# First expert unit: tokens chosen a tile earlier, rows turned inside attention's last two tiles, the end of routing spread over more steps

## The chip, the cores and the metric

The kernel runs on one core of one Trainium2 chip. The metric is the device time of one execution in microseconds (us); lower is better. The kernel before took 1397.6 us, the median of three runs from 1397.01 to 1399.13. One core has five instruction streams that work side by side: TensorE (PE, matmuls, with PEld for its weight loads), VectorE (DVE), ScalarE (ACT), GpSimd (POOL, which also issues the indirect DMAs) and SyncE (SP, which only issues DMAs). A trailing q, as in SPq or ACTq, marks an engine's own queue of issues and waits. Streams wait for each other by semaphores.

## The reference

Three layers, one after the other, on 4608 tokens of 512 numbers (8 batches of 576, 8 heads of 64):

```python
# 1: retention attention, no softmax
ret = (q @ k.T / 8) * Dmat          # Dmat[i,j] = gamma_head**(i-j) for i>=j, else 0
x   = (ret @ v), heads side by side # [4608, 512]
# 2: a mixture of 8 experts, one expert for each token
logits = x @ w_gate + modality_bias[modality_id]
e_idx  = argmax(logits); gate = softmax(logits)[e_idx]
y[tok] = gate * (relu(x[tok] @ w1[e]) @ w2[e])   # 512 -> 1024 -> 512
# 3: a dense block
h = y @ w_in; out = (h - tanh(h)) @ w_out        # 512 -> 2048 -> 512
```

## The kernel before

All matmuls carry fp32 in two pieces, a rounded high part and a low part, as three passes (high by high, high by low, low by high). There are three stages.

**Attention and routing.** The loop over t runs over 36 tiles of 128 tokens. The step of tile t issues scores(t+1) (L362; DVE masks the scores into `a`, L366), attend(t) (L398 with the carried state, L406 with `a` and the scaled values `vs` that POOL makes, L421 the new state, which ACT copies at L425), and evac_x(t) (DVE, L431), which puts the tile's output into `xt`, a buffer for a group of four tiles. Routing of a group g of four tiles comes in three parts, a tile apart, after the group is complete: route_a (logits on PE, L462, copied to `ls` by ACT, L465), route_b (transposes, L471, and the argmax on DVE, L475 to L487, into `oh_all`) and route_c (ranks, L496 to L501 on PE, then slots and counts on DVE, L504 to L514). Behind it, tile by tile, scatter writes the token numbers into a list of slots in DRAM (POOL, L517 and L518, tile `slot_d`), and store_x turns the rows (turn_x, L529), scales them (ACT, L534, tile `xo`) and writes them to `x_d` in DRAM (L536). `due` delays the scatters of group 6 so that they come in two halves.

**The first expert's tokens.** When seven of the nine groups are counted (EARLY = 7), choose() (L437 on PE, L441 to L453 on DVE) picks the expert with the most tokens so far. SP reads the pick into registers (L607, L608), load_ids (L199) reads 400 slot entries into `idt0`, and gather_rows (L203, POOL) fetches 128, 128, 128 and 16 rows of `x_d`, here into two buffers `vk` of the attention's pool. Once attention is done, turn_rows transposes each block of rows (L161 on PE into `sc` or `xp`), ACT writes the high part `xh` (L162) and DVE the low part `xl` (L163).

**Expert units.** A unit is 400 tokens of one expert, in eight steps f. A step has 12 matmuls of gemm1 (L712, 512 to 128 hidden) and, two steps behind, 12 of gemm2 (L933 to L935). The weights of a step come by DMA into `raw` (load_raw, L781), and split_w cuts them into `wh` (ACT, L790) and `wl` (DVE, L791). After gemm1 of a step, post() makes `hi` (ACT, L822) and `lo` (DVE, L823), splits the next weights and loads later ones, and then prep() does work that fills in. In unit 0 prep does the end of routing: rest_a at f = 0 (last scatters of group 7, route_b of group 8), rest_b at f = 1 (route_c of group 8, two late stores, four scatters), rest_c at f = 2 (L640, the counts summed; table(), L660 to L683, 23 small DVE instructions that lay out all further units; four late stores). Then swap() exchanges the buffer pools; SP reads the table, load_ids fetches the ids of unit 1 at f = 2, its rows are gathered at f = 3 (L203, tile `xg`) and turned at f = 6 and 7.

**Dense block.** From about 600 us to the end PE multiplies without a break.

Each engine runs its instructions in the order in which this code issues them. Memory is assigned by the order in which pools and tiles are opened: `raw` lies on bytes that the attention's `vk`, `vs` and `a` used.

Of the kernel before, what the change touches and what calls it, by code (L numbers as in the profile page):

```python
# [8 lines left out]
F32 = mybir.dt.float32  # L9
# [21 lines left out]
RG = 4  # L31
# [84 lines left out]
def kernel(tc, A, out):  # L116
    nc = tc.nc
    with ExitStack() as ctx:
# [132 lines left out]
        with tc.manual_schedule():  # L251
            c1, c1r = ExitStack(), ExitStack()
            p1, p1r = pools(c1), pools(c1r)
# [10 lines left out]
            ps_m = p1r("ps_m", 2, space=PSUM, side="right")  # L264
# [38 lines left out]

            load_tile(0)
# [268 lines left out]
            for t in range(NTILE):  # L573
                g, r = divmod(t, RG)
                if t + 1 < NTILE:
                    scores(t + 1)
                attend(t)
# [13 lines left out]
                if t >= RG + 3:  # L591
                    for w in due(t - RG - 3):
                        scatter(w)
                if g >= 1:
                    if r == 0:
                        ls_box[g - 1] = route_a(g - 1)
                    elif r == 1:
                        route_b(g - 1, ls_box.pop(g - 1))
                    elif r == 2:
                        route_c(g - 1)  # L600
# [3 lines left out]
                if t == (EARLY + 1) * RG - 1:  # L604
                    choose()
                if t == (EARLY + 1) * RG + 1:
# [4 lines left out]
                    x0 = [gld.tile([128, 2, DM], F32, name="vk") for _ in range(SE // 2)]  # L611
                    x0 = [x0[s // 2][:, s % 2] for s in range(SE)]
# [9 lines left out]
            def early(s):  # L622
                turn_rows(0, s, x0[s], ps_sc.tile([128, KD, TL], F32, name="sc") if s < 3 else ps_x.tile([128, 2, KD, TL], F32, name="xp")[:, 0])

            def rest_a():
                for i in range(3):
                    scatter(NTILE - RG - 3 + i)
                route_b(g, ls_last)
                save_x(t_ahead, tp_ahead, True)
                late_x(1)  # L630

            def rest_b():
                route_c(g)
                late_x(2)
                for r in range(RG):
                    scatter(g * RG + r)

            def rest_c():
                cp = ps_m.tile([128, E], F32, name="m")
                nc.tensor.matmul(out=cp, lhsT=ones, rhs=cum[:, NRG], start=True, stop=True)  # L640
                table(cp)
                late.extend(range(g * RG, NTILE))
                late_x(RG)
# [41 lines left out]
            early(0)  # L685
            early(1)
            ls_last = route_a(g)
            for s in range(2, SE):
                early(s)
            t_ahead = late.pop(0)  # L690
            tp_ahead = turn_x(t_ahead, False)
# [56 lines left out]
            with ExitStack() as c2:  # L748
# [69 lines left out]
                def post(i, hp, ht):  # L818
                    if hp is None:
                        return  # L820
                    hi, lo = (ht_p.tile([128, UL], F32R, name=n)[:, 0:UE] for n in ("hi", "lo"))
# [244 lines left out]
```

## Time and profile before

| | |
|---|---|
| runs | 1397.6 us median (1397.01 to 1399.13) |
| profiled execution | 1397.72 us, its span 1396.0 us |
| busy share of the span | PE 97%, DVE 75%, ACT 50%, POOL 24% |
| scores of the last tile begin / first gemm1 begins | 143.41 / 154.06 us |
| gemm1 of unit 0, step 3, ends / rows of unit 1 turned from | 172.31 / 185.28 us |

The profile is of one execution. Its page names the busy time of each engine, and the trace behind it gives the start, the length and the wait ahead of each instruction: `[0.67 <-ACT wh L790]` behind a row says that the engine sat idle for 0.67 us just before it, and that the last thing it waited for was ACT writing `wh` at line 790. Matmuls overlap by their fill, so a row's length is longer than the distance to the next row. Times in us count from the start of the span.

### The profile page before, as it was taken

The page shows a single profiled execution, that of the slowest core. Times are in us where ns is not written, and L with a number is a line of the kernel's source. Part 1 is how long each engine was busy: PE and PEld are TensorE (multiplying, and loading weights), DVE is VectorE, ACT ScalarE, POOL GpSimd, SP SyncE. Part 2 cuts the span into 40 slices and gives each one's busy share as a digit, 9 for nine tenths or more (in the row PEclk, how much of TensorE's full clock was granted, in tenths as well). Part 3 has the DMA queues.
Part 4 walks back from the last instruction along what each step waited for, and adds up shares of the span by engine and source line. Part 5 has one row for each costly group of instructions (what it writes and reads, how often), then busy time and mean ns, then how long its engine had stood idle before and what let it go on. Part 6 is the DMA issues. An engine that isn't in the chain of part 4 may idle for free.

```text
span 1396.0 us, 22342 instructions
## 1 busy us (share of the span) xinstructions
PE 1358.1 (97%) x8267; PEld 1185.8 (85%) x8267; DVE 1048.7 (75%) x1684; ACT 695.9 (50%) x1232; POOL 337.3 (24%) x381
## 2 busy tenths in 40 slices
PE   8999899999989999999999999999999999999998
PEld 7887798999989999988888888888888888888886
DVE  5766677888888888658878778787787877778775
ACT  3323444444434444446656555555555555565553
POOL 4555353343334444010011100111001110011101
PEclk9999999999999999999999999999999999999999
DMA  9997647444743336634000000000000000000000
GB/s 372 404 332 280 207 151 210 125 132 137 221 126 94 95 94 165 119 128 154 31 31 31 31 1 31 31 31 31 1 31 31 31 31 0 31 31 0 31 1 31
DMA packets 79858, 141.06 MB, mean 101 GB/s; under 512 B 36224, under 2 KB 42944, under 8 KB 79744
## 3 DMA queue, kind: packets, MB, share of 16 engines
q1 hardware_dynamic: 58912, 84.23, 19.3%
q10 hardware_dynamic: 12096, 35.45, 7.2%
q0 software_dynamic: 8736, 19.90, 4.5%
q8 instruction: 66, 1.08, 0.3%
q14 instruction: 48, 0.39, 0.1%
HBM read 133.33 MB, written 39.80 MB: 124 GB/s over the span
## 4 chain that ended last, share of the span: by engine, by line
PE 51%; issue 5%; POOL 0%; POOLq 0%; ACT 0%
PE hp L712 26%; PE acc L1010 8%; PE acc L1012 8%; PE acc L1011 8%; POOL out_dram L1036 0%; POOLq L1062 0%; ACT o L1033 0%; POOL nopt L1035 0%; POOLq L1026 0%; POOLq L1036 0%
## 5 line engine op out<-in xcount | busy, mean ns | idle before, releaser
L983 ACT ACTIVATE eh<-hp 128x512 f32<-128x512 f32 x144 | 86.4, 600 | 293.0 <-PE hp L712 276.0
L712 PE MATMUL hp<-xh,winh 128*128 128x512 f32 x576 | 224.2, 389 | 0.1
L1010 PE MATMUL acc<-wout,hi 128*128 128x512 f32 x576 | 224.2, 389 | 0.0
L1012 PE MATMUL acc<-wout,lo 128*128 128x512 f32 x576 | 224.2, 389 | 0.0
L1011 PE MATMUL acc<-wout,hi 128*128 128x512 f32 x576 | 224.1, 389 | 0.0
L712 PE MATMUL hp<-xh,winl 128*128 128x512 f32 x576 | 224.1, 389 | 0.0
L712 PE MATMUL hp<-xl,winh 128*128 128x512 f32 x576 | 224.1, 389 | 0.0
L985 DVE TENSOR_TENSOR el<-eh,hp 128x512 f32<-128x512 f32 x144 | 99.1, 688 | 156.4 <-ACT eh L984 156.4
L194 POOL DMA_INDIRECT xg<-x_d,idt x130 | 155.6, 1197 | 216.8 <-DVE cv_a L235 70.5
L740 POOL TENSOR_TENSOR xl<-yr,xh 128x512 fp32r<-128x512 f32 x36 | 49.2, 1367 | 429.7 <-ACT xh L739 429.7
L933 PE MATMUL acc<-hi,wh 128*128 128x400 f32 x384 | 132.6, 345 | 16.3 <-ACT yo L912 16.3
L994 DVE SCALAR_TENSOR_TENSOR el<-eh,el 128x512 f32<-128x512 f32 x144 | 128.5, 893 | 15.4 <-DVE el L993 0.5
L712 PE MATMUL hp<-xh,wl 128*128 128x400 f32 x384 | 133.2, 347 | 4.3 <-DVE wl L791 4.0
L791 DVE TENSOR_TENSOR wl<-raw,wh 128x1024 fp32r<-128x1024 f32 (+1 forms) x98 | 117.7, 1202 | 24.4 <-ACT wh L790 23.0
L712 PE MATMUL hp<-xh,wh 128*128 128x400 f32 x384 | 131.7, 343 | 1.2 <-ACT wh L790 0.7
L712 PE MATMUL hp<-xl,wh 128*128 128x400 f32 x384 | 131.5, 342 | 0.8 <-DVE xl L163 0.8
L934 PE MATMUL acc<-lo,wh 128*128 128x400 f32 x384 | 131.3, 342 | 0.0
L935 PE MATMUL acc<-hi,wl 128*128 128x400 f32 x384 | 131.3, 342 | 0.0
L712 PEld LDWEIGHTS hp<-xh,winh 128*128 128x128 f32 x576 | 108.2, 188 | 22.9 <-issue 0.5
L1012 PEld LDWEIGHTS acc<-wout,lo 128*128 128x128 f32 x576 | 108.1, 188 | 22.8 <-DVE lo L989 0.4
L1011 PEld LDWEIGHTS acc<-wout,hi 128*128 128x128 f32 x576 | 108.2, 188 | 22.5
L712 PEld LDWEIGHTS hp<-xh,winl 128*128 128x128 f32 x576 | 108.1, 188 | 22.6
(169 smaller groups left out, 2541.4 us busy)
## 6 DMA issues: line engine op xcount, KB each, us to landing
raw<-in_w_dram SPq DMA_DIRECT2D x91, 512.0 KB
qk<-in_qk_dram SPq DMA_DIRECT2D x36, 512.0 KB
vk<-in_vk_dram SPq DMA_DIRECT2D x36, 512.0 KB
y_d<-yo SPq DMA_DIRECT2D x12, 800.0 KB
yr<-y_d SPq DMA_DIRECT2D x9, 1024.0 KB
raw<-in_wo_dram ACTq DMA_DIRECT2D x16, 512.0 KB
wo_d<-cv_em ACTq DMA_DIRECT2D x16, 512.0 KB
raw<-in_wi_dram ACTq DMA_DIRECT2D x16, 512.0 KB
```

What stands on the lines that cost most here:

```text
L194: nc.gpsimd.indirect_dma_start(out=dst, out_offset=None, in_=x_d[0:NT, :].rearrange("t (q c) -> (t q) c", q=NQ), in_offset=bass.IndirectOf ...
L712: nc.tensor.matmul(out=hp, lhsT=lhs, rhs=rhs, start=j == 0, stop=j == 3 * KD - 1)
L791: nc.vector.tensor_tensor(out=wl[:, 0:n], in0=r, in1=wh[:, 0:n].bitcast(F32), op=ALU.subtract)
L933: nc.tensor.matmul(out=o, lhsT=wh[:, cs], rhs=hi, start=first, stop=False)
L934: nc.tensor.matmul(out=o, lhsT=wh[:, cs], rhs=lo, start=False, stop=False)
L935: nc.tensor.matmul(out=o, lhsT=wl[:, cs], rhs=hi, start=False, stop=last)
L983: nc.scalar.activation(out=u, in_=hp, func=ACTF.Square)
L985: nc.vector.tensor_tensor(out=v, in0=u, in1=hp, op=ALU.mult)
L994: nc.vector.scalar_tensor_tensor(out=v, in0=s, scalar=SQ_C, in1=v, op0=ALU.add, op1=ALU.mult)
L1010: nc.tensor.matmul(out=acc[s], lhsT=hi, rhs=wh, start=first, stop=False)
L1011: nc.tensor.matmul(out=acc[s], lhsT=hi, rhs=wl, start=False, stop=False)
L1012: nc.tensor.matmul(out=acc[s], lhsT=lo, rhs=wh, start=False, stop=last)
```

## The change

The chain for group 6 runs a tile earlier: route_a right behind scores(29) in the step of tile 28, route_b in that step, route_c at 29, the scatters two a tile at 29, 30 and 31 (the tile before brings one), choose() at 30 instead of 31, and the loads and gathers at 32 instead of 33. The rows go to a buffer `xt` instead of two `vk`. Their first block is transposed after scores(35) and before attend(34), the next two before attend(35), and the last, of 16 rows, after attention. In the opening of unit 0 the three raw loads come first, then split_w of step 0, the late turn_x, the last block of rows, route_a of group 8, and split_w of steps 1 and 2. rest_b moves from f = 1 to f = 2, with route_c of group 8 ahead of it in post() of that step; rest_c, swap and the ids of unit 1 move from f = 2 to f = 3; late stores are two each at f = 1, 2 and 3. The turning of unit 1's rows stays at f = 6 and 7. The pool `ps_m` has its own stack, `acc` is opened at f = 2, and two unused pairs of `qk` and `vk` tiles are allotted at the start.

```diff
@@ -249,8 +249,8 @@
             return load, [(COST[0], lambda: (p0(), p1())), (COST[1], p2), (COST[2], p3), (COST[3], p4)], save
 
         with tc.manual_schedule():
-            c1, c1r = ExitStack(), ExitStack()
-            p1, p1r = pools(c1), pools(c1r)
+            c1, c1r, c1m = ExitStack(), ExitStack(), ExitStack()
+            p1, p1r, p1m = pools(c1), pools(c1r), pools(c1m)
             att = p1("att", 1)
             gld = p1("gld", AHEAD)
             tmp = p1("tmp", 2)
@@ -261,7 +261,7 @@
             ps_sc = p1("ps_sc", 3, space=PSUM)
             ps_x = p1("ps_x", 1, space=PSUM)
             ps_st = p1("ps_st", 1, space=PSUM)
-            ps_m = p1r("ps_m", 2, space=PSUM, side="right")
+            ps_m = p1m("ps_m", 2, space=PSUM, side="right")
 
             mask = att.tile([128, 2, TL], F32, name="mask")
             gx = att.tile([128, PERIOD, H // 2, TL], F32, name="gx")
@@ -301,6 +301,9 @@
                 if w < TL:
                     nc.scalar.copy(out=gx[:, r, :, w:TL], in_=gx[:, 0, :, 0:TL - w])
 
+            for _ in range(AHEAD - 4):
+                gld.tile([128, 2, H // 2, TL], F32, name="qk")
+                gld.tile([128, 2, DM], F32, name="vk")
             load_tile(0)
             nc.gpsimd.memset(mask, 1.0)
             for m in range(2):
@@ -572,8 +575,16 @@
 
             for t in range(NTILE):
                 g, r = divmod(t, RG)
+                soon = g == EARLY
                 if t + 1 < NTILE:
                     scores(t + 1)
+                if soon and r == 0:
+                    ls_box[g - 1] = route_a(g - 1)
+                if t == NTILE - 2:
+                    turn_rows(0, 0, x0[0], ps_sc.tile([128, KD, TL], F32, name="sc"))
+                if t == NTILE - 1:
+                    for s in range(1, SE - 1):
+                        turn_rows(0, s, x0[s], ps_m.tile([128, KD, TL], F32, name="m"))
                 attend(t)
                 evac_x(t)
                 if t + 4 < NTILE:
@@ -588,28 +599,42 @@
                     make_gx(t + 1)
                 if 2 <= t < 5:
                     clear_slots(t - 2)
-                if t >= RG + 3:
-                    for w in due(t - RG - 3):
+                if t >= RG + 3 and not soon:
+                    w = t - RG - 3
+                    if w // RG != EARLY - 1:
                         scatter(w)
                 if g >= 1:
                     if r == 0:
-                        ls_box[g - 1] = route_a(g - 1)
+                        if not soon:
+                            ls_box[g - 1] = route_a(g - 1)
+                        else:
+                            route_b(g - 1, ls_box.pop(g - 1))
+                            scatter(t - RG - 3)
                     elif r == 1:
-                        route_b(g - 1, ls_box.pop(g - 1))
+                        if not soon:
+                            route_b(g - 1, ls_box.pop(g - 1))
+                        else:
+                            scatter(t - RG - 3)
+                            scatter(t - RG - 2)
+                            route_c(g - 1)
                     elif r == 2:
-                        route_c(g - 1)
+                        if not soon:
+                            route_c(g - 1)
+                    if soon and r >= 2:
+                        for w in range(t - RG - 2 + r - 2, t - RG + r - 2):
+                            scatter(w)
                     for w in due(t - RG - 2):
                         if w // RG < NRG - LATE:
                             store_x(w)
-                if t == (EARLY + 1) * RG - 1:
+                if t == EARLY * RG + 2:
                     choose()
-                if t == (EARLY + 1) * RG + 1:
+                if t == (EARLY + 1) * RG:
                     base = nc.sync.value_load(pick[0:1, 0:1], min_val=0, max_val=(E - 1) * CAP)
                     first = nc.sync.value_load(pick[0:1, 1:2], min_val=0, max_val=E - 1)
                     first_act = nc.scalar.value_load(pick[0:1, 1:2], min_val=0, max_val=E - 1)
                     load_ids(base, idt0)
-                    x0 = [gld.tile([128, 2, DM], F32, name="vk") for _ in range(SE // 2)]
-                    x0 = [x0[s // 2][:, s % 2] for s in range(SE)]
+                    x0 = xt_p.tile([128, SE, DM], F32, name="xt")
+                    x0 = [x0[:, s] for s in range(SE)]
                     for s in range(SE):
                         gather_rows(s, idt0, x0[s], EARLY * RG * TL)
             g = NRG - 1
@@ -619,28 +644,26 @@
                 for _ in range(min(n, len(late))):
                     store_x(late.pop(0), True)
 
-            def early(s):
-                turn_rows(0, s, x0[s], ps_sc.tile([128, KD, TL], F32, name="sc") if s < 3 else ps_x.tile([128, 2, KD, TL], F32, name="xp")[:, 0])
-
-            def rest_a():
+            def rest_a(ls, t, tp):
                 for i in range(3):
                     scatter(NTILE - RG - 3 + i)
-                route_b(g, ls_last)
-                save_x(t_ahead, tp_ahead, True)
+                route_b(g, ls)
+                save_x(t, tp, True)
                 late_x(1)
 
             def rest_b():
-                route_c(g)
-                late_x(2)
                 for r in range(RG):
                     scatter(g * RG + r)
+                late.extend(range(g * RG, NTILE))
+                late_x(RG // 2)
+                c1m.close()
+                P["acc"] = pool("acc", 4, space=PSUM, side="right")
 
             def rest_c():
-                cp = ps_m.tile([128, E], F32, name="m")
+                cp = P["hp"].tile([128, UB], F32, name="hp")[:, 0:E]
                 nc.tensor.matmul(out=cp, lhsT=ones, rhs=cum[:, NRG], start=True, stop=True)
                 table(cp)
-                late.extend(range(g * RG, NTILE))
-                late_x(RG)
+                late_x(RG // 2)
 
 
             def table(cp):
@@ -682,13 +705,6 @@
                 ts(out=utab[:, 2], in0=ue, scalar1=float(NT), scalar2=None, op0=ALU.min)
                 nc.vector.tensor_copy(out=nreg, in_=incl[:, E - 1:E])
 
-            early(0)
-            early(1)
-            ls_last = route_a(g)
-            for s in range(2, SE):
-                early(s)
-            t_ahead = late.pop(0)
-            tp_ahead = turn_x(t_ahead, False)
             c1.close()
             wres = pool("wres", 1)
             winh = wres.tile([128, F3, DM], F32R, name="winh")
@@ -819,10 +835,12 @@
                     if hp is None:
                         return
                     hi, lo = (ht_p.tile([128, UL], F32R, name=n)[:, 0:UE] for n in ("hi", "lo"))
+                    if steps[i] == (0, 2):
+                        route_c(NRG - 1)
                     nc.scalar.activation(out=hi, in_=hp, func=ACTF.Relu)
                     nc.vector.scalar_tensor_tensor(out=lo, in0=hp, scalar=0.0, in1=hi.bitcast(F32), op0=ALU.max, op1=ALU.subtract)
                     ht[i] = (hi, lo)
-                    split_w((i, 1), (i + 2, 0))
+                    split_w((i, 1), *[(i + 2, 0)][(i + 2, 0) in wsp:])
                     load_raw(i + F1)
                     if steps[i] in ((0, 0), (0, 1)):
                         for f in range(3 * i + 3, min(F1, 3 * i + 6)):
@@ -836,6 +854,7 @@
 
                 yr0 = [None]
                 idts = {}
+                ahead = []
 
                 def swap():
 
@@ -843,7 +862,6 @@
                     po, pr = pools(ctx), pools(c2)
                     po("line", 1, side="right").tile([128, PAD // 4], F32, name="line")
                     P["yr"], P["wo"] = (po(n, 1, side="right") for n in ("yr", "wo"))
-                    P["acc"] = po("acc", 4, space=PSUM, side="right")
                     P["id"] = pr("id2", 1, side="right")
                     P["yo"] = pr("yo2", 1, side="right")
                     cv2 = pr("cv2", 1, side="right")
@@ -862,13 +880,15 @@
                     if u == "t":
                         return
                     if u == 0 and f == 0:
-                        rest_a()
+                        rest_a(*ahead)
                     if u == 0 and f == 1:
+                        late_x(2)
+                    if u == 0 and f == 2:
                         rest_b()
-                    if u == 0 and f == 2:
+                    if u == 0 and f == 3:
                         rest_c()
                         swap()
-                    for v, g in ((1, 2), *((v, 4) for v in range(TURNED, UMIN))):
+                    for v, g in ((1, 3), *((v, 4) for v in range(TURNED, UMIN))):
                         if (u, f) == (max(v - 2, 0), g):
                             idts[v] = ids_of(v)
                         if (u, f) == ((0, 3) if v == 1 else (v - 2, F1 - 1)):
@@ -945,7 +965,16 @@
                             turn_blocks(names[0], s, xg[names[0]])
                             split_high(names[0], s, xg[names[0]])
                             split_low(names[0], s, xg[names[0]])
-                    split_w((1, 0))
+                        split_w((1, 0))
+                    else:
+                        for _ in range(2):
+                            h_p.tile([128, UB], F32, name="hp")
+                        t = late.pop(0)
+                        tp = turn_x(t, True)
+                        turn_rows(0, SE - 1, x0[SE - 1], h_p.tile([128, UB], F32, name="hp").rearrange("p (k t) -> p k t", k=KD))
+                        ahead.extend((route_a(g), t, tp))
+                        split_w((1, 0))
+                        split_w((2, 0))
                     blocks(names, F1, 2, UE, xT, lambda i: None, g1w, gemm2e, post, prep, finish)
 
                 run_units(range(UMIN), None)
```

Lines of the changed kernel are numbered three higher early on (L362 becomes L365), and more later (L712 becomes L728, L781 L797, L790 and L791 L806 and L807, L823 L841, L640 L664, L660 L683).

POOL, before, from the scaling of the last tile's values (`vs` of tile 35) to the gathers of the first unit's rows:

```order
L372 TENSOR_TENSOR vs<-vk,small 128x512
L517 MEMSET nopt 128x1
L518 DMA slot_d<-tokid,pos_s 37376x16
L517 MEMSET nopt 128x1
L518 DMA slot_d<-tokid,pos_s 37376x16
L517 MEMSET nopt 128x1
L518 DMA slot_d<-tokid,pos_s 37376x16
L517 MEMSET nopt 128x1
L518 DMA slot_d<-tokid,pos_s 37376x16
L203 DMA vk<-x_d,idt_69 128x512 x3
L203 DMA vk<-x_d,idt_69 16x512
```

POOL, of the change, the same stretch:

```order
L375 TENSOR_TENSOR vs<-vk,small 128x512
L520 MEMSET nopt 128x1
L521 DMA slot_d<-tokid,pos_s 37376x16
L520 MEMSET nopt 128x1
L521 DMA slot_d<-tokid,pos_s 37376x16
L203 DMA xt<-x_d,idt_69 128x512 x3
L203 DMA xt<-x_d,idt_69 16x512
```

Two of the four scatters that stood between `vs` of tile 35 and the gathers now stand ahead of that `vs`, and the rows land in `xt`.

PE, before, from the end of the ranks of group 7 to the first gemm1 (`sc<-ident,vk` and `xp<-ident,vk` are the transposes of the first unit's rows):

```order
L501 MATMUL m<-cum,ones 128x32
L398 MATMUL xp<-qk,state_112 64x128 x8
L406 MATMUL xp<-a,vs 64x128 x8
L161 MATMUL sc<-ident,vk 128x128 x8
L462 MATMUL m<-xt,wg 32x512 x4
L161 MATMUL sc<-ident,vk 128x128 x4
L161 MATMUL xp<-ident,vk 128x16 x4
L529 MATMUL m<-ident,xt 128x128 x4
L712 MATMUL hp<-xh,wh 128x400
L712 MATMUL hp<-xl,wh 128x400
L712 MATMUL hp<-xh,wl 128x400
```

PE, of the change: the scores of tile 35, the first block of rows, and attend(34) behind it:

```order
L365 MATMUL sc<-qk 128x128 x8
L161 MATMUL sc<-ident,xt 128x128 x4
L401 MATMUL xp<-qk,state_113 64x128 x8
L409 MATMUL xp<-a,vs 64x128 x8
L424 MATMUL st<-vs,vk 64x64 x8
```

PE, of the change: the end of the ranks of group 7 to the first gemm1:

```order
L504 MATMUL m<-cum,ones 128x32
L161 MATMUL m<-ident,xt 128x128 x8
L401 MATMUL xp<-qk,state_112 64x128 x8
L409 MATMUL xp<-a,vs 64x128 x8
L532 MATMUL hp<-ident,xt 128x128 x4
L161 MATMUL hp<-ident,xt 128x16 x4
L465 MATMUL m<-xt,wg 32x512 x4
L728 MATMUL hp<-xh,wh 128x400
L728 MATMUL hp<-xl,wh 128x400
L728 MATMUL hp<-xh,wl 128x400
```

Twelve of the sixteen transposes of rows moved from behind attend(35) to ahead of it, four of them ahead of attend(34); between attend(35) and the first gemm1 stay the four turns of a late store, the four small transposes and the logits of group 8.

DVE, before, from the low part of gemm1 of step 2 (`lo`, the next weights `wl`) into the table:

```order
L823 SCALAR_TENSOR_TENSOR lo<-hp,hi 128x400
L791 TENSOR_TENSOR wl<-raw,wh 128x1024
L660 COPY vals<-m 1x8
L661 TENSOR_TENSOR scs<-vals,mio 1x96
L662 TENSOR_REDUCE vals<-scs 1x8
L663 TENSOR_TENSOR scs<-vals,tri 1x64
L664 TENSOR_REDUCE incl<-scs 1x8
L665 TENSOR_TENSOR ls<-incl,uio 1x152
```

DVE, of the change, the low part of gemm1 of step 2 too:

```order
L841 SCALAR_TENSOR_TENSOR lo<-hp,hi 128x400
L807 TENSOR_TENSOR wl<-raw,wh 128x1024
L841 SCALAR_TENSOR_TENSOR lo<-hp,hi 128x400
L807 TENSOR_TENSOR wl<-raw,wh 128x1024
L683 COPY vals<-hp 1x8
L684 TENSOR_TENSOR scs<-vals,mio 1x96
L685 TENSOR_REDUCE vals<-scs 1x8
L686 TENSOR_TENSOR scs<-vals,tri 1x64
```

The table now stands behind `lo` and `wl` of step 3 as well.

## Rows read from the trace of the kernel before

**Rows 1.** Windows, PE alone: length, busy (instructions), granted clock, DMA share, GB/s.

```profile
132.00:200.00 68.00, 62.45 (x580) 1.00 0.51 163
600.00:1350.00 750.00, 749.85 (x3315) 1.00 0.10 35
```

**Rows 2.** Timeline of POOL: start, length, line, operation, tiles [idle before <-releaser].

```profile
134.05 1.04 POOL L372 TENSOR_TENSOR vs<-vk,small 128x512 f32<-128x512 f32 x1 [1.91 <-PE st L421]
...
139.12 0.96 POOL L518 DMA_INDIRECT slot_d<-tokid,pos_s  x1 [0.19 <-issue]
144.16 0.99 POOL L203 DMA_INDIRECT vk<-x_d,idt  x1 [4.08 <-DMA idt<-slot_d]
145.45 0.96 POOL L203 DMA_INDIRECT vk<-x_d,idt  x1 [0.31 <-issue]
```

**Rows 3.** Timeline of SP: when its DMAs are issued.

```profile
141.49 0.42 SPq L199 DMA_DIRECT2D idt<-slot_d  x1
149.02 1.55 SPq L781 DMA_DIRECT2D raw<-in_w_dram  x3
...
173.50 0.40 SPq L199 DMA_DIRECT2D idr<-slot_d  x1
```

**Rows 4.** What the trace says of line 203, all eight gathers.

```profile
DMA to landing us min/median/max: 4.1/4.4/4.7
```

**Rows 5.** Timeline of PE from the last scores to the first gemm1's end.

```profile
143.41 1.16 PE L362 MATMUL sc<-qk 64*128 64x128 f32 x16
144.50 0.67 PE L398 MATMUL xp<-qk,state 64*64 64x128 f32 x16
...
147.18 0.67 PE L398 MATMUL xp<-qk,state 64*64 64x128 f32 x16 [0.30 <-ACT state L425]
148.81 0.66 PE L161 MATMUL sc<-ident,vk 128*128 128x128 f32 x4
149.93 0.66 PE L161 MATMUL sc<-ident,vk 128*128 128x128 f32 x4 [0.47 <-DMA vk<-x_d,idt]
150.52 1.07 PE L462 MATMUL m<-xt,wg 128*32 128x512 f32 x8
...
152.41 0.39 PE L161 MATMUL xp<-ident,vk 16*128 16x16 f32 x4 [0.24 <-DMA vk<-x_d,idt]
152.73 0.66 PE L529 MATMUL m<-ident,xt 128*128 128x128 f32 x4
154.06 0.45 PE L712 MATMUL hp<-xh,wh 128*128 128x400 f32 x1 [0.67 <-ACT wh L790]
...
156.71 0.60 PE L471 MATMUL m<-ident,ls 128*128 128x128 f32 x4
```

**Rows 6.** Waits of PE: waited for, us in total, times, longest.

```profile
PE m L496 <- DVE oh_all L487: 1.3, 1, 1.3
PE m L640 <- DVE cum L510: 0.8, 1, 0.8
...
PE hp L712 <- ACT xo L534: 0.5, 1, 0.5
```

**Rows 7.** Timeline of PE in unit 0, from step 2 on.

```profile
165.43 1.95 PE L529 MATMUL hp<-ident,xt 128*128 128x128 f32 x16
...
172.31 0.34 PE L933 MATMUL acc<-hi,wh 128*128 128x400 f32 x1
...
185.28 1.03 PE L161 MATMUL hp<-ident,xg 128*128 128x128 f32 x8
```

**Rows 8.** Timeline of DVE: the table's ends, and the split behind it.

```profile
167.38 0.15 DVE L660 COPY vals<-m 1x8 f32<-1x8 f32 x1
...
172.50 0.13 DVE L683 CAST nreg<-incl 1x1 int32<-1x1 f32 x1
...
173.99 1.23 DVE L791 TENSOR_TENSOR wl<-raw,wh 128x1024 fp32r<-128x1024 f32 x1 [0.36 <-ACT wh L790]
```

**Rows 9.** Timeline of PE: the first scores of the kernel.

```profile
4.99 2.08 PE L362 MATMUL sc<-qk 64*128 64x128 f32 x16 [4.99 <-DMA qk<-in_qk_dram]
```

## The prediction

> **What bounds the kernel now.** I read the page's shares first, then PE alone in windows, then PE's waits, then the timelines of the engines it waits for. The windows decide where to look: from 600 to 1350 us PE is busy for 749.85 of 750.00 us, so whatever reaches that stage late ends the kernel late by as much [rows 1]. The change touches 132 to 200 us, where PE is busy 62.45 of 68.00 us at a granted clock of 1.00 [rows 1]. That leaves 5.55 us of idle time, and since the change neither adds nor drops matmuls, no more than about 5.5 us can be won. The question is which idle goes and which comes.
>
> **Up to the last scores.** The routing of group 6 and choose() are the same instructions a tile earlier, among attention's matmuls; I cost them at nothing, and let scores(35) end at 144.50 as before [rows 5]. DVE and POOL have gaps there; if that cover failed, it would be some tenths.
>
> **The gathers, term 1.** Before, POOL scales the last `vs` at 134.05 for 1.04 us, then issues four scatters, the last at 139.12; ids are loaded at 141.49, 2.37 later; the first gather is issued at 144.16, 2.67 later [rows 2, 3]. It lands in 4.4 us (4.1 to 4.7) [rows 4], so at about 148.6, just before PE first turns its rows at 148.81 [rows 5]: covered. After, two scatters stand behind that `vs`, at a pitch like that of the gathers, 145.45 - 144.16 = 1.29 [rows 2]: 2.6 us sooner, less 0.3 for a choose() that now lies ahead of `vs`. Last scatter 136.9, ids 139.3, gather 141.9, landing 146.3. But the first block is now turned at 144.5, and PE takes instructions in order: attend(34) and all behind it wait. Stall: 146.3 - 144.5 = 1.8; I take 2.0, since choose() may cost POOL as much as its 0.5 of matmul and wait. The later gathers land 1.3 us apart and are turned only after attend(34): no further wait. Bounds from the landings seen: 1.5 to 2.3.
>
> **The turns, term 2.** Twelve transposes come ahead of attend(35). A block of four takes 150.52 - 149.93 = 0.59, so 1.77; the 0.30 wait for the state disappears behind them [rows 5]. Attention's end: 148.81 + 2.0 + 1.77 - 0.30 = 152.3.
>
> **The weights, term 3.** Here the words "into other memory" have to be checked. The changed program still puts the first `raw` tile on bytes of the last `vk`, `vs` and `a`, and its load still waits for the last matmuls of attend(35). The trace of before agrees with that place: last block of attention ends at 148.81, load issued at 149.02 [rows 3, 5]. So it is issued at 152.5. From issue to the first gemm1 matmul took 154.06 - 149.02 = 5.04, to that gemm1's end another 156.71 - 154.06 = 2.65 [rows 3, 5]. Before, 12 of the turns plus the logits filled that time; after, PE has one late turn, the last 16 rows and the logits, about 0.6 + 0.3 + 1.0 = 1.9 by the distances of rows 5. The rest of 157.5 - 152.3 = 5.2, some 3.3 us, is new idle time. The second matmul also waits for the 16 rows' `xl`, which DVE now makes behind the first `wl`: not seen before; between 0 and 0.67, the wait that stood at this gemm1 [rows 5]; I take 0.2, as the pieces are small. gemm1 of step 0 ends at 160.4, against 156.71: **+3.7**.
>
> **Unit 0, term 4.** Three of PE's waits go, because rank and counts now have a step more: 1.3 for `oh_all`, 0.8 for `cum`, 0.5 for `xo` [rows 6], together -2.6. The late stores at f = 1 put a new wait for `xo` ahead of gemm1 of step 2: 0 to 0.8 by the waits of that kind, 0.5 by the nearest row: **-2.1** net. Eight of the 16 turns that took 1.95 us at f = 2, about 1.0 us, move behind step 3 [rows 7]: no change in the sum, but it sets the distances of the next term. From the end of gemm1 of step 3 to unit 1's turns: 185.28 - 172.31 = 13.0 before, 14.0 after [rows 7].
>
> **The second gather, term 5.** The table now starts behind `lo` and `wl` of step 3. In the trace that `wl` ends at 173.99 + 1.23 = 175.2, which is 2.9 after gemm1's end at 172.31; the table takes 172.50 + 0.13 - 167.38 = 5.25 [rows 7, 8]. Ids follow 173.50 - 172.63 = 0.87 later [rows 3, 8], the gather 2.67 after them as above, and it lands in 4.4. So, counted from the end of gemm1 of step 3: 2.9 + 5.25 + 0.87 + 2.67 + 4.4 = 16.1 for the first block, 17.4 for the second. PE is there at 14.0 and does both blocks in one go of some 0.8: it would be done at 14.8, and is done at 17.4 + 0.3 = 17.7. Stall **+2.9** (bounds 2.4 to 3.3 by the landings). Before, the table was done 12.6 us ahead of that place; the turning did not move with it.
>
> **Sum.** 3.7 - 2.1 + 2.9 = 4.5 us on the profiled 1397.72; that execution stands 0.1 above the median, so 1397.6 + 4.4 = 1402.0. No term lies beside another: each delays PE, and all that follows is PE's.
>
> **Two rules of the Trainium skill.** The eight gathers took 4.1 to 4.7 us to land [rows 4]. "DMA: Bandwidth & Descriptors", section "Anatomy of one DMA — SWDGE (gpsimd) path", gives a fixed 2.0 us and the bytes at 436 GB/s; for 256 KB that is an estimate of 2.6 us, under which terms 1 and 5 would lose 1.8 us each and the sum would be about +0.9. No gather here came near it.
> The first scores of the kernel took 2.08 us, later ones 143.41 to 144.50, 1.09 a tile, at a granted clock that reads full in the windows [rows 1, 5, 9]. "TensorE: Matmul & The Clock Gate", section "HAM oscillation — how this bites in real kernels", says that waits for DMA between bursts drop the engine to half speed and let the next burst start slow; it is the second rival below.
>
> **Rivals.**
> 1. *The waits are shorter than their nearest rows; no change (0.18).* Either gathers land as soon as the ids' load let the first gather go, 2.67 us [rows 2, 3], which leaves 4.5 - 2 x 1.7 = +1.1, or the load of `raw` is free before attention ends, which takes term 3's 3.3 us away and leaves about +1.2: 1398.7. For it: two DMA streams that were busy together (DMA share 0.51) [rows 1] are further apart. Against: the shortest of eight landings is 4.1, and the load's place in the order.
> 2. *Slow restart (0.06, inside slower).* PE idles 2.0, 3.3 and 2.9 us at three places; if it then runs at the pace of its first scores, 2.08 against 1.09 [rows 5, 9], a gemm1 of 2.65 costs up to 2.4 us more, and I count one to two such bursts: 1404.4 to 1406.5. Against: before, waits up to 1.3 us left no slow rows, and the granted clock reads 1.00 [rows 1, 6]; a stop of 3.3 us has no row.
> 3. *Faster (0.14).* All loads of the first unit are hidden: weights issued at least 3.3 us before attention ends and rows there when PE turns to them. Then terms 1, 3 and 5 lose 2.0, 3.3 and 2.9, leaving 4.5 - 8.2 = -3.7: 1393.9. It decides from the point where the first `raw` is issued ahead of attend(35) and each gather is issued two to three us sooner than I count. For it: four waits of before end on DMA or on what was loaded; against: terms 1, 3 and 5.
>
> **The numbers.** Forecast as summed 0.62, of its own range 1400.3 to 1403.6 (terms 1, 3, 4, 5 at their ends, not all at once); with rival 2 slower is 0.68. Within 0.2%, or 2.8 us, which is about what a measurement of this kernel can tell: 0.18. Faster: 0.14. Range 1395.5 to 1404.5: it takes in the forecast, the no-change cases and the edge of the faster one.
>
> **What would show it.** In the changed profile: the first transposes `sc<-ident,xt` with about 2 us of idle time that ends on the gather; the first `raw` issued right behind attend(35), near 152.5; the first gemm1 with over 3 us of idle time on `wh`; the waits on `oh_all` and `cum` gone; unit 1's turns with about 3 us on the gather. PE idle in the corresponding 132 to 204 us would be some 10 us. The prediction is wrong if `raw` is issued while attention still runs, if the rows are there when PE reaches them, or if PE's turns of unit 1 find theirs; it is wrong upwards if matmuls behind a stall run at half pace.

## The result

The changed kernel took 1408.85 us, the median of five runs from 1407.29 to 1413.99; the kernel before, on the same chip, 1397.6 (five runs, 1396.78 to 1399.13). The ratio is 1.0085 with a 95% interval of 1.0065 to 1.0105: slower by some 11 us, where 4.4 were forecast, and outside the range, which ended at 1404.5. The profiled execution took 1407.29 us with a span of 1405.6, 9.6 longer than that of before.

The waits of PE in the changed kernel, from 130 to 215 us (waited for, us in total, times, longest), answer to [rows 6]:

```profile
PE hp L161 <- DMA xg<-x_d,idr: 3.5, 2, 2.6
PE sc L161 <- DMA xt<-x_d,idt: 2.7, 1, 2.7
PE hp L728 <- ACT xh L162: 2.3, 1, 2.3
```

The waits on `oh_all` and `cum` and the one of gemm1 on `xo` are gone, and the three that were forecast are there: the first unit's rows, the first weights (by way of `xh`, which stands behind their split on ACT), and unit 1's rows. ACT shows the second of them:

```profile
157.81 0.62 ACT L806 CAST wh<-raw 128x512 fp32r<-128x512 f32 x1 [4.63 <-DMA raw<-in_w_dram]
158.34 0.21 ACT L162 CAST xh<-hp 128x64 fp32r<-128x64 f32 x1
```

But these waits are only half of it. Windows of PE from the last scores to the first matmul of unit 1 (length, busy with instructions, granted clock, DMA share, GB/s), first of before and then of after, with the stretches up to the first gemm1, that gemm1, up to the end of step 3, up to unit 1's turns, and the rest:

```profile
143.41:193.58 50.17, 45.79 (x352) 1.00 0.59 188
```

```profile
143.21:202.46 59.25, 50.31 (x352) 0.91 0.49 159
143.21:158.59 15.38, 10.18 (x130) 0.89 0.41 125
158.59:162.73 4.14, 3.96 (x12) 0.59 0.33 125
162.73:174.68 11.95, 11.88 (x79) 1.00 0.85 294
174.68:188.77 14.09, 14.09 (x82) 1.00 0.48 165
188.77:202.46 13.69, 10.20 (x52) 0.88 0.34 83
```

The same work, 352 records of PE in both, takes 59.25 us instead of 50.17, 9.08 more (the first window ends 0.06 us short of unit 1's first matmul, at 193.64). Idle time went from 50.17 - 45.79 = 4.38 to 59.25 - 50.31 = 8.94, by 4.56. Busy time went from 45.79 to 50.31, by 4.52, for the same matmuls. Unit 1 begins 8.8 us later than before, since the last scores begin 0.2 us earlier; the other 0.8 us of the 9.6 comes later. Single microseconds of the changed kernel (same columns) show when:

```profile
147.00:148.00 1.00, 0.89 (x16) 1.00 0.66 217
148.00:149.00 1.00, 1.00 (x23) 0.76 0.71 205
149.00:150.00 1.00, 1.00 (x14) 0.50 0.28 88
...
151.00:152.00 1.00, 1.00 (x10) 0.54 0.00 0
152.00:153.00 1.00, 1.00 (x21) 1.00 0.00 0
...
159.00:160.00 1.00, 0.83 (x3) 0.50 0.82 329
...
193.00:194.00 1.00, 1.00 (x5) 0.50 0.12 39
194.00:195.00 1.00, 1.00 (x5) 0.50 0.00 0
...
196.00:197.00 1.00, 1.00 (x7) 0.85 0.00 0
```

Behind each of the three waits the granted clock falls to 0.50, the lower of its two levels (1.2 of 2.4 GHz), for three to four us, and comes back while PE works without a break. The timeline of PE shows what that does to a row (start, length, line, operation [idle before <-releaser]):

```profile
147.11 0.63 PE L161 MATMUL sc<-ident,xt 128*128 128x128 f32 x4 [2.74 <-DMA xt<-x_d,idt]
...
148.26 1.78 PE L409 MATMUL xp<-a,vs 128*64 128x128 f32 x16
...
153.03 1.09 PE L409 MATMUL xp<-a,vs 128*64 128x128 f32 x16
154.06 0.66 PE L532 MATMUL hp<-ident,xt 128*128 128x128 f32 x4
...
158.59 0.58 PE L728 MATMUL hp<-xh,wh 128*128 128x400 f32 x1 [2.26 <-ACT xh L162]
...
159.85 0.54 PE L728 MATMUL hp<-xh,wl 128*128 128x400 f32 x1
...
162.37 0.34 PE L728 MATMUL hp<-xl,wh 128*128 128x400 f32 x1
...
191.39 0.66 PE L161 MATMUL hp<-ident,xg 128*128 128x128 f32 x4 [2.62 <-DMA xg<-x_d,idr]
192.91 1.11 PE L161 MATMUL hp<-ident,xg 128*128 128x128 f32 x4 [0.87 <-DMA xg<-x_d,idr]
193.68 0.68 PE L953 MATMUL acc<-hi,wh 128*128 128x400 f32 x1
```

The same a·v block of a tile takes 1.78 us at 148.26 and 1.09 at 153.03; a matmul of 400 columns 0.54 us and then 0.34.

Not every wait of that length is followed by half clock, though. Later in the same profile, and once in the kernel before, PE waits as long for a low part of weights, `wl`, and the windows that hold these waits and the work behind them read 1.00 (first the changed kernel, then the one before):

```profile
399.50 0.45 PE L728 MATMUL hp<-xh,wl 128*128 128x400 f32 x1 [2.95 <-DVE wl L807]
399.00:404.00 5.00, 2.86 (x14) 1.00 0.56 149
```

```profile
390.22 0.45 PE L712 MATMUL hp<-xh,wl 128*128 128x400 f32 x1 [2.35 <-DVE wl L791]
390.00:395.00 5.00, 3.15 (x16) 1.00 0.58 170
```

So these traces don't tell from the length of a wait alone whether the clock falls behind it. The loads themselves, on SP and on POOL:

```profile
140.79 0.42 SPq L199 DMA_DIRECT2D idt<-slot_d  x1
154.27 1.44 SPq L797 DMA_DIRECT2D raw<-in_w_dram  x3
...
183.04 0.40 SPq L199 DMA_DIRECT2D idr<-slot_d  x1
```

```profile
136.97 0.96 POOL L521 DMA_INDIRECT slot_d<-tokid,pos_s  x1 [0.19 <-issue]
143.50 0.99 POOL L203 DMA_INDIRECT xt<-x_d,idt  x1 [5.58 <-PE m L474]
...
187.37 1.00 POOL L203 DMA_INDIRECT xg<-x_d,idr  x1 [11.34 <-DVE wl L807]
```

The first raw load is issued at 154.27, right behind attention's last block, which began at 153.03 and is followed at 154.06: the first weights are not loaded earlier than before. The last scatter is where the forecast put it, 136.97, but the ids follow 3.8 us later instead of 2.4 [rows 2, 3], as SP waits for that scatter to land, so the gather goes out at 143.50, not 141.9.

### The profile page after: what moved, and what is told of

Same layout as the page of the kernel before. It is cut to its first block, busy times and chain, and to the rows that moved or that the text cites. A ratio compares the mean times of both kernels' runs of the same rounds, so it can differ in the third digit from the quotient of the medians.

```text
span 1405.6 us, 22353 instructions
## 1 busy us (share of the span) xinstructions
PE 1362.1 (97%) x8267; PEld 1189.4 (85%) x8267; DVE 1049.8 (75%) x1685; ACT 696.5 (50%) x1233; POOL 332.4 (24%) x381
## 4 chain that ended last, share of the span: by engine, by line
PE 50%; issue 5%; POOL 0%; POOLq 0%; ACT 0%
PE hp L728 25%; PE acc L1040 8%; PE acc L1039 8%; PE acc L1041 8%; POOL out_dram L1065 0%; POOLq L1091 0%; ACT o L1062 0%; POOL nopt L1064 0%; POOLq L1055 0%; POOLq L1065 0%
## 5 line engine op out<-in xcount | busy, mean ns | idle before, releaser
L728 PE MATMUL hp<-xh,winh 128*128 128x512 f32 x576 | 224.1, 389 | 0.1
L728 PE MATMUL hp<-xh,winl 128*128 128x512 f32 x576 | 224.1, 389 | 0.0
L728 PE MATMUL hp<-xl,winh 128*128 128x512 f32 x576 | 224.1, 389 | 0.0
L194 POOL DMA_INDIRECT xg<-x_d,idt x130 | 152.0, 1169 | 219.0 <-ACT hi L840 54.3
L807 DVE TENSOR_TENSOR wl<-raw,wh 128x1024 fp32r<-128x1024 f32 (+1 forms) x99 | 117.9, 1190 | 28.3 <-ACT wh L806 26.6
L728 PE MATMUL hp<-xh,wl 128*128 128x400 f32 x384 | 133.6, 348 | 5.3 <-DVE wl L807 4.9
L728 PE MATMUL hp<-xh,wh 128*128 128x400 f32 x384 | 132.2, 344 | 2.3 <-ACT xh L162 2.3
L728 PE MATMUL hp<-xl,wh 128*128 128x400 f32 x384 | 132.2, 344 | 0.4 <-DVE xl L163 0.4
L728 PEld LDWEIGHTS hp<-xh,winh 128*128 128x128 f32 x576 | 108.1, 188 | 22.9 <-issue 0.5
L728 PEld LDWEIGHTS hp<-xh,winl 128*128 128x128 f32 x576 | 108.2, 188 | 22.6
```

The costliest lines, as they stand in the source:

```text
L194: nc.gpsimd.indirect_dma_start(out=dst, out_offset=None, in_=x_d[0:NT, :].rearrange("t (q c) -> (t q) c", q=NQ), in_offset=bass.IndirectOf ...
L728: nc.tensor.matmul(out=hp, lhsT=lhs, rhs=rhs, start=j == 0, stop=j == 3 * KD - 1)
L807: nc.vector.tensor_tensor(out=wl[:, 0:n], in0=r, in1=wh[:, 0:n].bitcast(F32), op=ALU.subtract)
```

## The experiments

Theory A: three waits of PE on loads, and behind each the matmuls run at half clock; half of the loss is the one, half the other. Rival B: the idle time alone costs, and the slow rows have another cause. Rival C: what is won at one load is waited for at the next. Three more chips took part, one for each group of runs. On all three the kernel before itself takes 1406 to 1407 us, so each kernel is told by its ratio to the kernel before of its own chip. Of each edit only the lines that carry it are shown.

**The two kernels again.** Unchanged.

> The kernel before, unchanged, for a profile beside the other runs of the same chip. Where a chip gives 1397 to 1399 us, the waits of the first profile come back; where it gives some 1407, the extra 9 us should stand in the trace as stalls that the first profile lacks, at places that all kernels have in common.

> The changed kernel, unchanged, against the kernel before on the same chip as the experiments. Theory A (the three stalls and the half clock behind them belong to the program): 8 to 12 us slower than before, whatever the chip's own level. Rival D (the difference is one of chips or of executions): within 3 us of before on this chip.

> The changed kernel again, on the chip of the next three runs, as what they are compared with. Theory A: slower than before, 3 to 11 us as on the two chips so far, with half clock behind each of the three loads that PE waits for.

The kernel before had 1407.78 us in the profiled run. The changed kernel: 1410.49 us on that chip, ratio 1.0025 (1.0014 to 1.0036), and 1411.44 us on the third, ratio 1.0029 (1.0020 to 1.0038). So its own level hardly moved from chip to chip, 1408.85 to 1411.44; what moved is the kernel before, and the loss there is 4 us, not 11. Theory A's 8 to 12 us whatever the chip was a miss, and rival D's 3 us or less was one too. The timeline of PE in the kernel before on that chip shows where it lost time that the first profile does not have:

```profile
138.80 0.38 PE L406 MATMUL xp<-a,vs 128*64 128x128 f32 x2 [0.42 <-issue]
...
140.95 0.61 PE L421 MATMUL st<-vs,vk 128*64 128x64 f32 x13 [0.50 <-issue]
...
150.52 0.60 PE L406 MATMUL xp<-a,vs 128*64 128x128 f32 x6 [0.89 <-issue]
...
160.82 0.70 PE L712 MATMUL hp<-xh,wh 128*128 128x400 f32 x1 [2.17 <-ACT wh L790]
160.00:164.00 4.00, 3.18 (x9) 0.57 0.30 120
```

PE stops amid a tile's matmuls with nothing that the profile names as awaited. The scores of the last tile start at 146.25 there, against 143.41 [rows 5], and ahead of the first gemm1 stands a wait of 2.17 us for the first weights, with half clock behind it (the last line is a window): on this chip the kernel before has such a stall of its own. At the end of gemm1 of step 0 the two kernels are level, 164.59 and 164.47 us; unit 1 begins at 200.75 and 205.23, behind the changed kernel's waits for unit 1's rows and their slow matmuls. In the changed kernel on that chip the stops add up to only 0.8 us, and the wait on the first rows is 1.1 us instead of 2.7, as its last scores start 0.9 later and its gather goes out 0.5 earlier than in the first profile; the clock does not fall behind it. On the third chip that wait is 1.1 us too, again with no fall, where half clock was expected behind all three loads. What the stops are is open.

The granted clock of whole runs says the same. Its median is 0.996 and 0.995 for the kernel before on the chips where both kernels ran, and 0.993 for the changed kernel on both, where the first profile of the kernel before had 0.999. Of 1410 us, 0.002 to 0.003 is an estimated 3 to 4 us: most of what the changed kernel loses there.

**Filling the stalls.** Nothing but spare transposes in front of the three waits, so that PE isn't idle in them:

```diff
+        def keep_busy(tp, n):
+            for i in range(n):
+                nc.tensor.transpose(tp[:, i % KD], ident, ident)
...
+                    keep_busy(sc0, 16)       # ahead of turn_rows(0, 0, ...)
+                        keep_busy(idle, 14)  # ahead of the first gemm1
+                        keep_busy(tp, (16, 4)[s])  # ahead of unit 1's first two blocks
```

> The changed kernel with spare transposes of the identity on PE, 16, 14 and 16 + 4 of them, issued just ahead of the three places where PE stood idle on a load (first unit's rows, first weights, unit 1's rows). Theory A (each stall costs its idle time and then a stretch of matmuls at half clock, together some 4.3 us: 1.35 + 1.3 + 1.65): the granted clock stays at 1.00 through 145 to 200 us and the time falls by about 4 us, to 1404 to 1405. Rival B (the clock falls for another cause than the idle engine, or the slow rows cost nothing on the path): clock below 1.00 as before in the same places, time within 1 us of 1408.8.

> The changed kernel with the spare transposes of fill_stalls, now beside the changed kernel on one chip. The stalls stay as long as they are, only PE isn't idle in them. Theory A (half clock behind the stalls costs some 4.3 us): 3 to 5 us faster than the changed kernel of this chip. Rival B (idle time alone): within 1 us of it.

The first run gave 1405.81 us, ratio 0.9990 (0.9977 to 1.0003), on a chip on which the changed kernel was not run; its granted clock reads 1.00 all through 140 to 200 us. Beside the changed kernel: 1408.43 against 1411.44 us, ratio 1.0004 (0.9992 to 1.0016) against 1.0029. Some 3 us come back though the kernel does more work and waits for the same loads; the intervals don't touch. The granted clock of the runs rises with it, from a median of 0.993 to 0.997, an estimated 5.6 us of 1410; why only 3 of them show in the time is open. Windows behind unit 1's rows, of the changed kernel and of the filled one on that chip:

```profile
190.00:195.00 5.00, 2.42 (x14) 1.00 0.63 126
195.00:200.00 5.00, 4.26 (x17) 0.66 0.15 44
```

```profile
190.00:195.00 5.00, 3.88 (x29) 1.00 0.48 85
195.00:200.00 5.00, 4.68 (x30) 1.00 0.30 84
```

The clock stays up where PE was kept busy: rival B falls. In the filled kernel's profile on that chip two slow stretches are left: 0.57 from 156 to 164 us, behind a wait of 2.85 us at the end of attention that no spare transposes stand in front of, and 0.57 from 252 to 260, behind one of 2.80 us in a later gemm1. That profile is of the slowest of its twelve runs, 1412.47 us, no faster than the changed kernel's profiled run, 1412.14. So what the half clock costs is shown in kind; its size there, 3 us, is that of medians, and the single profiles don't divide it among the places.

**The first block of rows a tile later.**

```diff
-                if t == NTILE - 2:
-                    turn_rows(0, 0, x0[0], ps_sc.tile(...))
                 if t == NTILE - 1:
-                    for s in range(1, SE - 1):
+                    for s in range(SE - 1):
```

> The changed kernel with the first block of rows turned with the next two, ahead of attend(35), not ahead of attend(34). Theory A: the gather lands at about 147.1 as now, PE is there at 146.6, so the stall of 2.7 us shrinks to about 0.5 and the slow matmuls behind it go (1.35): 3.5 us faster than the changed kernel, 1405. Rival B (stall only, clock elsewhere): 2.2 faster. Rival C (the time is set by the weights' load or the table, and what is won here is waited for there): no change.

1412.42 us, ratio 1.0034 (1.0022 to 1.0046): a miss, no better than the changed kernel on other chips (1.0025, 1.0029). The wait on the gather is gone, but PE in attend(34) and behind attend(35):

```profile
148.17 0.43 PE L409 MATMUL xp<-a,vs 128*64 128x128 f32 x2 [0.96 <-issue]
149.60 0.60 PE L409 MATMUL xp<-a,vs 128*64 128x128 f32 x6 [1.00 <-issue]
...
158.92 0.42 PE L161 MATMUL hp<-ident,xt 16*128 16x16 f32 x4 [2.92 <-DVE xt L434]
```

The place that waited for rows now stops for "issue", by 2.0 us, and the later loads are waited for longer than in the changed kernel on the two other chips: 2.2 us on `xh` (1.0 and 1.2 there) and 3.9 on `xg` (3.2 and 3.3). This is what rival C says, in part with a load and in part with stops that no load explains. The changed kernel was not run on this chip, and a chip without such stops was not tried.

**Unit 1's rows a step later.**

```diff
-                    if u == 0 and f >= 6:
-                        for s in range(2 * f - 12, 2 * f - 10):
+                    if u == 0 and f == 7:
+                        for s in range(SE):
```

> The changed kernel with all four blocks of unit 1's rows turned at step 7 of unit 0, not two at 6 and two at 7. Theory A: the waits of 2.6 and 0.9 us on the gather go, with the slow matmuls behind them (1.65); a new wait of 0.3 to 0.8 for the last low part ahead of unit 1: 4 to 5.5 us faster, about 1404. Rival C (what is won is waited for ahead of unit 1's first gemm1, whose operands come later): 0 to 1.5 us faster.

1406.77 us, ratio 1.0002 (0.9986 to 1.0017), against 1.0025 and 1.0029 of the changed kernel on the other chips: about 3.5 us less, just under the 4 to 5.5 expected. No wait on `xg` is left in its trace, and the clock reads 1.00 from 170 us on. But it is at 0.50 from 148 to 151 and from 159 to 168 us, and the median clock of its runs, 0.993, is that of the changed kernel: what was won is waiting, and the slow time did not shrink with it. The comparison goes across chips, so its size is rough.

**The end of routing put back.**

```diff
-                    if u == 0 and f == 1:
-                        late_x(2)
-                    if u == 0 and f == 2:
+                    if u == 0 and f == 1:
                         rest_b()             # with route_c(8) in it again
-                    if u == 0 and f == 3:
+                    if u == 0 and f == 2:
                         rest_c()
```

> The changed kernel with the end of routing put back: route_c of group 8, late stores and scatters at step 1, the table and unit 1's ids at step 2; the early choice and the turning inside attention stay. Theory A: the waits for oh_all, cum and xo come back (2.6), the stall on unit 1's rows (3.5) and its slow matmuls (1.65) go: 2 to 3.5 us faster than the changed kernel. Rival E (spreading the end of routing is the part that pays, the early turns the part that costs): 2 to 3 us slower than the changed kernel.

1408.77 us, ratio 1.0004 (0.9993 to 1.0016), 2.7 us less than the changed kernel beside it, as theory A said; rival E falls. Of the waits that were to come back only the one on `cum` did, 1.0 us, and none on `xg` is left. Spreading the end of routing over one more step costs more at unit 1's rows than the waits it removes.

**The first weights in a tile of their own.**

```diff
-                raw = raw_p.tile([128, 2 * F1, DM], F32, name="raw")
+                raw0 = raw_p.tile([128, 2, DM], F32, name="raw0")
+                raw1 = raw_p.tile([128, 2 * F1 - 2, DM], F32, name="raw")
```

> The changed kernel with the raw weights of step 0 as a tile of their own, on bytes that only the values of tiles 32 and 33 used, so that its load does not wait for attend(35); the splits of steps 0 and 2, 7 and 8 are apart where they were joined. Theory A: the load is issued near 141 us instead of 154.3, the wait of 2.3 us ahead of the first gemm1 shrinks to under 1 and the half clock behind it (1.3) goes: 3 to 3.6 us faster, about 1405.5. Rival C (the load is not what ends that wait, the small last block's high part is): no change.

1419.82 us, ratio 1.0086 (1.0065 to 1.0107): a miss, and the worst of all. The load did go out early, at 144.59 us, the first split of weights began at 154.40 and took 0.63 us, and the wait ahead of the first gemm1 is gone. But splits that were joined now took two buffers each, of three, at every change of unit, and new waits came at unit 1, which I put down to that (not tried apart):

```profile
205.57 0.45 PE L728 MATMUL hp<-xh,wh 128*128 128x400 f32 x1 [1.59 <-ACT xh L162]
...
222.20 0.70 PE L957 MATMUL acc<-hi,wh 128*128 128x400 f32 x1 [2.75 <-ACT yo L936]
```

The next kernels keep one buffer for such a pair and copy its two halves apart.

**Two and three moves together.** two_moves is rows_later with unit1_later; three2 adds the first weights in a tile of their own:

```diff
+                        for w, r in cuts:
+                            nc.scalar.copy(out=wh[:, w], in_=r)
```

> The changed kernel with the first block of rows turned ahead of attend(35) instead of attend(34), and all of unit 1's rows turned at step 7. Theory A: stalls one and three go with their slow matmuls: 6 to 8 us faster than the changed kernel; the wait for the first weights (2.3 us) and its slow matmuls stay. Rival C (each gain is waited for at the next load): under 3 us faster.

> As two_moves, and the raw weights of step 0 as a tile of their own whose load does not wait for attend(35), without the extra weight buffers of the earlier form. Theory A: no stall of over 1 us on a load is left in 130 to 210 us and the granted clock stays at 1.00: 9 to 12 us faster than the changed kernel, 0 to 3 us faster than the kernel before. Rival C: no better than two_moves.

> three2 again, to see whether it also beats the kernel before on another chip. Theory A: 2 to 5 us faster than before, 6 to 9 faster than the changed kernel. If its lead of the other chip came only from what that chip lost in the kernel before, within 1 us of before.

Beside the changed kernel with 1410.49 us, two_moves took 1406.1 (ratio 0.9995, 0.9986 to 1.0004) and three2 1402.9 (0.9971, 0.9962 to 0.9981): the two moves took 4.4 us away and the three 7.6, both less than expected (6 to 8 and 9 to 12). On the third chip three2 took 1408.63 us, ratio 1.0012 (1.0000 to 1.0023): 2.8 us less than the changed kernel, not the 6 to 9 expected, and no better than the kernel before. Its trace on the first of these chips has no wait of PE over 1 us on a load left from 130 to 230 us, as expected, but the clock is at 0.50 from 157 to 163 us, and these waits stand there:

```profile
PE hp L161 <- DVE xt L434: 2.8, 1, 2.8
PE st L424 <- issue: 1.7, 3, 1.1
PE m L161 <- DMA xt<-x_d,idt: 0.8, 1, 0.8
```

A wait of 2.5 to 2.9 us at the end of attention stands in every trace of the changed kernel and its variants on the three later chips, named "issue" or the last `xt`, and not in the first one (0.2). It comes from DVE, whose last evac_x begins behind 1.9 to 3.0 us of idle time in each of them, here in the changed kernel on the second chip:

```profile
155.68 0.69 DVE L434 TENSOR_TENSOR xt<-xp,gx 128x512 f32<-128x512 f32 x1 [2.52 <-remote]
```

In the first profile this idle time is 0.17 us. What "remote" is, no run shows. The clock falls behind that wait in most of these traces, not in all: in three2_c, after 2.61 us, and in the first filled run, after 2.85, it stays at 1.00. A version that beats both kernels on every chip was not found.

## Why the prediction was right and wrong

- The direction, and the reason for it, came out: PE waits for three loads that it did not wait for before, in the places named. Idle time rose by 4.56 us in the stretch; the sum of the forecast, all of it idle time and moved work, was 4.5. That the two agree so closely is luck: the terms below miss by up to a microsecond each, in both directions, and cancel.
- Term 1, gather: 2.74 against 2.0. The ids' load waited 3.8 us behind the last scatter, not 2.4; the rows were quick, 143.50 to 147.1, 3.6.
- Term 3, weights: the load's place was right (154.27, right behind attention), its size was less: 4.32 us from issue to the first gemm1, not 5.04, and 2.26 us idle, not 3.3. Still that gemm1 ended at 162.73, not at 160.4: attention ended at 154.06 instead of 152.3, and the gemm1 itself took 1.49 us longer than before. The order argument against "into other memory" held.
- Term 4: from the end of gemm1 of step 0 to that of step 3 11.95 us, where 12.5 were forecast. The new wait for `xo` did not come.
- Term 5, unit 1's rows: 2.62 + 0.87 = 3.5 against 2.9. The table ended at 182.64, 8.0 us after step 3's gemm1 at 174.68, as worked out (2.9 + 5.25); the ids were asked for at once, but the gather went out 4.3 us after them, not 2.7.
- **The step that failed is the sum's rule that a stall costs its idle time.** "If it then runs at the pace of its first scores" stood as rival 2 with 0.06, "against: before, waits up to 1.3 us left no slow rows". The three stalls, 2.74, 2.26 and 2.62 with 0.87, are longer than any wait in that stretch of before, and behind each of them PE ran at half clock; that is the other 4.52 us. The rival's price for one burst, up to 2.4 us, was an upper bound: the first gemm1 took 4.14 instead of 2.65, 1.49 more. Its count of one to two bursts was too low; there were three. Its chance was too low as well: the row against it, 1.3 us, was shorter than any of the stalls that were forecast. The traces do not make it certain either, as the 2.35 us at 390.22 of the kernel before show, a row that the prediction did not look at.
- "TensorE: Matmul & The Clock Gate", section "HAM oscillation — how this bites in real kernels", of the Trainium skill, says that waits for DMA between bursts of matmuls let the engine fall to half clock. The trace agrees at these three places: 0.50 behind each. It does not agree behind the 2.95 us at 399.50.
- That rows land as fast as the fixed cost and bandwidth of "DMA: Bandwidth & Descriptors", section "Anatomy of one DMA — SWDGE (gpsimd) path", of the Trainium skill was held to be unlikely, and rightly: 3.6 us for the first gather here.
- The median is 1.6 us above the profiled run, whose clock was the best of the five, 0.996 against 0.991 to 0.995. What the others lost beyond it has no trace.
- That the loss shrinks to 4 us on the two later chips where both kernels ran is not a vindication of the 4.4: the kernel before loses time there that it does not lose here.
- Slips in the working, none of which decides anything: 4.5 us on 1397.6 is 1402.1, not 1402.0; two bursts of 2.4 make 1406.8, not 1406.5; and 2.08 is a row's length while 1.09 is a distance between rows. The later row's length is 1.16 [rows 5], which makes the price of a burst 2.1 us.

## What to carry to other kernels

Price a new stall of TensorE at its idle time, and give the slow matmuls behind it a price and a real chance of their own. Here they cost about as much again, 4.52 beside 4.56 us. The length of the stall doesn't settle it: waits of 2.35 and 2.95 us in these kernels left the clock full, and waits of 2.17 and 2.26 did not. Removing one stall need not give its slow time back either, as the clock may fall behind the next. A unit of work that is moved ahead of its load turns a hidden transfer into a stall; look for where the consumer stands, not only how early the load goes. Where a tile is one allocation, its load waits for all the bytes under it, so "other memory" has to be read from what the load waits for.

## What was not expected

- The same kernel differs by 0.7% between chips (1397.6 on one, 1406.4 to 1407.4 on three), with PE stops that the profile gives to "issue"; the changed kernel differs by 0.2%.
- Spare transposes in a wait are not wasted: 50 of them made the kernel 3 us faster on the one chip where both were run.
- In the first profile the clock reading did not fall while PE was idle, but 0.2 to 1.5 us after it had resumed: 1.00 in 147 to 148, 0.76 and then 0.50 from 148 on. That is no rule: in the changed kernel on the second chip it was already falling from 155 to 156 us (0.92), with PE idle until 156.43.
